# A two-layer attention and MLP kernel on one core: a new table of numbers for the planner that orders its instructions

## The chip, the cores and the metric

One Trainium2 chip, one NeuronCore. The metric is the device time of one execution in microseconds (us). The engines are named as the profile names them: PE (TensorE matmuls), PEld (TensorE weight loads), DVE (VectorE), ACT (ScalarE), POOL (GpSimd) and SP (SyncE, which issues DMAs).

## The reference

Two layers that share their weights, on x of 2048 rows by 448 columns in bf16. Each layer is an attention with 16 heads of 28 columns, and an MLP of 1792 hidden columns with a squared ReLU:

```python
def _A_ref(x, wqkv, wo):
    qkv = (x @ wqkv).reshape(B, S, 3, H, Dh).transpose(2, 0, 3, 1, 4)
    q, k, v = qkv[0], qkv[1], qkv[2]
    scores = jnp.einsum("bhqd,bhkd->bhqk", q, k) * Dh ** -0.5
    p = _softmax(scores, axis=-1)
    o = jnp.einsum("bhqk,bhkd->bhqd", p, v)
    return o.transpose(0, 2, 1, 3).reshape(B, S, D) @ wo

def _B_ref(x, w1, b1, w2, b2):
    r = relu(jnp.einsum("bsd,df->bsf", x, w1) + b1)
    return jnp.einsum("bsf,fd->bsd", r * r, w2) + b2

x = A_x
x = x + _A_ref(_layernorm(x), A_wqkv, A_wo)
x = x + _B_ref(_layernorm(x), B_w1, B_b1, B_w2, B_b2)
x = x + _A_ref(_layernorm(x), A_wqkv, A_wo)
x = x + _B_ref(_layernorm(x), B_w1, B_b1, B_w2, B_b2)
```

## The kernel before, in words

**The unit of work.** The exponentials are the bulk. The 2 x 16 x 2048 x 2048 scores are cut into 2048 *banks* of 128 keys (partitions) by 512 query columns in float32. The queries go in *blocks* of 256 rows; in the second layer the last 256 rows are two blocks of 128, here called block 7 and block 8. A *pass* is one block with one group of four heads, and each pass goes over all keys.

**Score groups.** `s_stream` issues a *score group*: up to three banks in one tile `sc` (two such tiles take turns), by matmuls of K_sb with Q_sb at L1360. Each bank of a group is of another head and so of other rows of the PE. ACT turns the banks of a group into `pt` with one ACTIVATE at L1403 (1536 columns for three banks, 1024 for two).

**Banks on DVE.** `apart` may give a bank to DVE. Usually it is the third one of a group, and then ACT gets two. A tile `sc` is free for a new group when ACT and DVE have both read it. DVE takes an exponential by integer arithmetic: one TENSOR_SCALAR out of `sc` (L1424, in `a_unit`), two *shifts* of what it made (L1440, in `a_rest`) and one addition (L1453). A shift may go to POOL or to DVE; `a_rest` names both engines, and the planner takes the one on which it would end first, with a handicap for DVE that numbers of the table set:

```python
t = Op(("POOL", "DVE"), (EDUR, TDUR), apiece, deps=[c], ...)
h = Op(("POOL", "DVE"), (EDUR, TDUR), other, deps=[c], ...)
t.aside = h.aside = lambda: TASIDE2 if pool_left[0] > PLIM or ... else TASIDE
```

A bank can also be a fourth one beside a group that keeps all three for ACT. It then lies in `mt`, one of the two PSUM tiles that the other matmuls use, and this is tried only when enough of them are free (`bank_free`, with the number MFREE):

```python
if len(us) == 3 and bank_free(o.start):
    j = apart(use(js), o.start, us, 0.0)      # own = True: four banks
if j is None and len(us) == 3 and THIRD:
    own = False                               # two for ACT, one for DVE
```

**The rest of the work**, on PE and DVE, lies between the score groups: `p_stream` multiplies `pt` by V_sb into `oT` (L1555); DVE and small DMAs divide by the row sums (L1625 to L1683); `chain` does the output projection (wo), the layernorm (L692, L697, L816, with a reciprocal root on POOL at L717), its transposes on PE (L756, copied by DVE at L768), the MLP (matmuls with w1 and w2 at L871, ReLU at L1763 on DVE or L1761 on ACT, square at L1770 or L1768, the sum to x at L1692), and for the first layer the second layer's K, Q and V (`qkv`, DVE at L972, L976 and L1006). A matmul with few rows can ride beside a score group in rows that it leaves free (L954). Where PE has room, a score group's matmuls are issued again, or an idle matmul (L1821) is put in.

**What sets the order.** A `Planner` runs when the program is built. It keeps a clock for each engine, takes at every step the operation that could start first (by priorities where several could), and so writes one fixed order for each engine. The chip only follows this order; waits are by semaphores. The planner's rules read some 60 numbers (C_PRIO, V_LATE, TASIDE, MFREE, MORE and so on). `s_stream` changes them on the way, at the score group whose number stands in the table `PACE`:

```python
gi = len(gbuf)
globals().update(PACE.get(gi, {}))
```

FORCE and SKIP in the table name single groups in which a bank must or must not go to DVE.

Of the kernel before, what the change touches and what calls it, by code (L numbers as in the profile page):

```python
# [180 lines left out]
SKIP = ()
PACE = {
    0: {'BUSY': 1.0, 'LOW': 0.7, 'CHUNK': 1, 'EV': 2.9, 'FAR': 6, 'KEEP': 5, 'LAG': 16, 'LEAD': 18, 'MARGIN':
         1.5, 'MORE': 3, 'PRE': 0.5, 'SLACK': 0.7, 'SPAN': 8, 'TB': 1.3, 'TB2': 3, 'V_AGE': 5, 'V_LAST': 3,
# [6 lines left out]
    16: {'PRE': 0, 'CHUNK': 3, 'PWAIT': 3},
    24: {'ASIDE': 0, 'TASIDE': 0.2, 'SKIP': (25,)},
    32: {'FORCE': (38,)},
    40: {'PLIM': 2, 'TASIDE': -0.2, 'XMIN': 3, 'SKIP': (47,)},
# [1 line left out]
    56: {'PWAIT': 0.6, 'V_LATE': 6},
    72: {'C_PRIO': 1.6},
    80: {'LOW': 0.5},
    88: {'TB': 1.6},
    96: {'CHUNK': 1, 'FORCE': (103,)},  # L200
    104: {'LEAD': 6},
    120: {'LAG': 1, 'SKIP': (120,)},
    128: {'CHUNK': 3, 'SKIP': (130,)},
    136: {'MARGIN': 3},
    160: {'SKIP': (161,)},
    168: {'GUEST': 1, 'FORCE': (172,)},
    176: {'GWAIT': 0.3, 'FORCE': (182,)},
    184: {'MMC': 0.46, 'SKIP': (185,)},
    192: {'GUEST1': 1, 'SKIP': (193,)},
    208: {'PMAX': 4, 'SKIP': (213,)},  # L210
    216: {'GNEXT': 0.3},
    232: {'PLIM': 4, 'FORCE': (239,)},
    240: {'GOPEN': 2},
    248: {'GUEST1': 0, 'FORCE': (253,)},
    264: {'FORCE': (270,)},
    272: {'NEAR_U': 0},
    288: {'SPARE': 5},
    296: {'PORTP': 2},
    304: {'LADD': 0.05, 'FORCE': (310,)},
    312: {'FORCE': (312,)},  # L220
    320: {'SKIP': (323,)},
    328: {'LADD': 0.1},
    336: {'HOLD': 3},
    352: {'PORTP': 0.3},
    360: {'GNEXT': 0.5, 'FORCE': (362,)},
    368: {'NEAR_U': 9, 'SKIP': (371,)},
    376: {'GWAIT': 1, 'PORTP': 0.1, 'SKIP': (383,)},
    392: {'PLIM': 2, 'FORCE': (394,)},
    400: {'BUSY': 1.05, 'V_PAST': 1, 'FORCE': (403,)},
    408: {'GUEST': 0},  # L230
    416: {'V_WAIT': 8},
    440: {'MORE': 1, 'FORCE': (445,)},
    448: {'TASIDE2': 0},
    456: {'TB2': 2.4},
    464: {'HOLD': 4, 'FORCE': (464,)},
    480: {'LADD': 0.2, 'BEHIND': 6},
    488: {'HOLD': 5, 'V_AGE': 3, 'PLIM': 6},
    496: {'C_PRIO': 2.6, 'RES': 1, 'PRE': 0.8},
    504: {'HOLD': 6, 'SPARE': 3, 'TASIDE': 0.2},
    512: {'FORCE': (515,)},  # L240
    520: {'NEAR': 3, 'SKIP': (524,)},
    528: {'V_AGE': 8, 'FORCE': (531,)},
    536: {'GOPEN': 0.2, 'FORCE': (536,)},
    552: {'BUSY': 1.0, 'FORCE': (556,)},
    560: {'VGAP': 0.08, 'GUEST': 1},
    568: {'LOW': 1.0},
    576: {'TB2': 3, 'FORCE': (581,)},
    584: {'V_PAST': 2, 'TB2': 1.6, 'V_WAIT': 3},
    592: {'RES2': 2, 'SOON': 0.3, 'FORCE': (594,)},
    600: {'FAR': 9, 'ASIDE': 0.2, 'FORCE': (605,)},  # L250
    608: {'GOPEN': 2, 'FORCE': (608,)},
    616: {'FAR': 6, 'FORCE': (619,)},
    624: {'V_LAST': 2.5},
    632: {'LAG': 3, 'RES': 3},
    648: {'MMC': 0.9},
    656: {'TASIDE2': -0.4},
# [1618 lines left out]
```

## Time and profile before

| | |
|---|---|
| three runs | 798.44, 799.81, 800.02 us; median 799.81 |
| the profiled execution | 799.5 us; its span from the first to the last instruction 797.7 us |
| busy in the span | PE 775.0, DVE 731.9, ACT 779.7, POOL 443.9 us |
| score groups on ACT (L1403) | 683: 318 of three banks, 365 of two |
| first group starts, last group ends on ACT | 9.58 us, 779.93 us |
| granted TensorE clock | 1.000 |

The profiled execution's own time is 1.8 us more than its span. A group's "busy" counts overlapping instructions once, and "mean ns" is the record of one instruction. Records of neighbours on DVE and on ACT overlap by some 0.1 us, so a record is longer than what an instruction costs in a full queue.

### The profile page before, as it was taken

Reading aid. Unit: us, or ns where it says so; the run is one execution under the profiler, and the core shown is the slowest. Engines: PE = TensorE matmul, PEld = TensorE weight load, DVE = VectorE, ACT = ScalarE, POOL = GpSimd, SP = SyncE. Lnnn points to the kernel's source line nnn. Section 1 sums busy time; section 2 is a strip of 40 time slices with the busy share of each in tenths; the row PEclk is TensorE's granted clock in tenths of the full one; section 3 lists DMA queues with packets and bytes.
Section 4 is the critical chain, followed back from the end, with each engine's and each line's share of the span. In section 5 each row is a group of like instructions: output and inputs, shape, how many; then the busy total and the mean of one; then the engine's idle time right before and its main releaser. Section 6 shows DMA issues by size and latency. Waiting matters only on the chain.

```text
span 797.7 us, 29438 instructions
## 1 busy us (share of the span) xinstructions
PE 775.0 (97%) x12386; PEld 418.1 (52%) x12386; DVE 731.9 (92%) x1673; ACT 779.7 (98%) x702; POOL 443.9 (56%) x704
## 2 busy tenths in 40 slices
PE   9999999999999999999999999989999999999998
PEld 6455545455454555455454544545454545555565
DVE  8899999989998979989998999899999999999663
ACT  8999999999999999999999999999999999999993
POOL 3365775745665645666665556465664565655310
PEclk9999999999999999999999999999999999999999
DMA  9200011000000000000000000011100000000000
GB/s 252 85 3 2 3 30 29 16 18 9 12 14 16 17 16 16 5 14 16 2 3 2 2 3 2 4 43 30 28 17 22 22 28 16 28 8 22 23 7 25
DMA packets 32482, 18.16 MB, mean 23 GB/s; under 512 B 17818, under 2 KB 31899, under 8 KB 32348
## 3 DMA queue, kind: packets, MB, share of 16 engines
q1 hardware_dynamic: 32204, 16.16, 7.3%
q8 instruction: 97, 1.59, 0.8%
q14 instruction: 37, 0.30, 0.1%
q10 hardware_dynamic: 144, 0.11, 0.0%
HBM read 13.98 MB, written 2.06 MB: 20 GB/s over the span
## 4 chain that ended last, share of the span: by engine, by line
PE 60%; DVE 17%; ACT 14%; issue 6%; DMA 1%; POOL 1%; ACTq 0%; SPq 0%; DVEq 0%; POOLq 0%
PE mt L871 26%; PE sc L1360 18%; ACT pt L1403 14%; PE oT L1555 13%; DVE pt L1424 5%; DVE pt L1453 2%; DVE r L1763 2%; PE mt L954 1%; PE tp L756 1%; DVE st L692 1%; PE sc L871 1%; DVE V_sb L1770 1%; DVE x_sb L1692 1%; DVE xn L816 1%; PE mt L890 1%
## 5 line engine op out<-in xcount | busy, mean ns | idle before, releaser
L1403 ACT ACTIVATE pt<-sc 128x1536 bf16<-128x1536 f32 (+1 forms) x683 | 767.1, 1261 | 3.8 <-PE sc L1360 2.7
L1360 PE MATMUL sc<-Q_sb,K_sb 32*128 32x256 bf16 (+1 forms) x4018 | 249.3, 268 | 12.2 <-ACT pt L1403 8.6
L1440 POOL TENSOR_SCALAR v_c<-pt 128x512 int16<-128x512 int16 x233 | 153.2, 658 | 96.6 <-DVE pt L1424 40.0
L1424 DVE TENSOR_SCALAR pt<-sc 128x512 int16<-128x512 f32 x277 | 188.7, 684 | 11.3 <-PE sc L1360 9.1
L1360 PEld LDWEIGHTS <-K_sb 32*128 32x128 bf16 x4700 | 102.2, 92 | 169.4 <-issue 102.0
L1555 PE MATMUL oT<-pt,V_sb 128*32 128x256 bf16 (+1 forms) x4168 | 184.7, 268 | 0.4
L1555 PEld LDWEIGHTS <-V_sb 128*32 128x32 bf16 x5104 | 119.1, 96 | 52.6 <-issue 48.7
L871 PE MATMUL mt<-xnT,w 128*128 128x256 bf16 (+1 forms) x904 | 120.7, 269 | 1.9 <-DVE xnT L768 1.0
L1440 POOL TENSOR_SCALAR K_sb<-pt 128x512 int16<-128x512 int16 x117 | 76.9, 657 | 60.2 <-DVE pt L1424 29.9
L871 PEld LDWEIGHTS <-w 128*128 128x128 bf16 x936 | 75.9, 97 | 37.7 <-issue 29.9
L1763 DVE TENSOR_SCALAR r<-mt 128x512 bf16<-128x512 f32 x106 | 72.4, 683 | 5.1 <-PE mt L871 4.4
L1440 POOL TENSOR_SCALAR V_sb<-pt 128x512 int16<-128x512 int16 x86 | 56.3, 654 | 32.5 <-DVE pt L1424 14.5
L1555 PE MATMUL oT<-v_c,V_sb 128*32 128x256 bf16 (+1 forms) x460 | 68.9, 271 | 0.1
L1453 DVE TENSOR_TENSOR pt<-pt,v_c 128x512 bf16<-128x512 bf16 x146 | 62.6, 437 | 2.2 <-POOL v_c L1440 1.8
L871 PE MATMUL mt<-w,V_sb 128*128 128x448 bf16 (+1 forms) x274 | 64.2, 350 | 0.0
L717 POOL TENSOR_TENSOR rstd<-mv,mhalf 128x2 f32<-128x2 f32 (+1 forms) x34 | 23.8, 700 | 38.2 <-DVE mv L699 21.2
L1440 POOL TENSOR_SCALAR v_c<-v_c 128x512 int16<-128x512 int16 x39 | 26.0, 668 | 25.3 <-DVE v_c L1424 13.9
L692 DVE BATCH_NORM_STATS2 st<-x_sb 128x6 f32<-128x448 bf16 x63 | 38.7, 615 | 0.8 <-DMA x_sb<-in_A_x_dram 0.6
L1692 DVE TENSOR_TENSOR x_sb<-x_sb,mt 128x448 bf16<-128x448 bf16 x60 | 36.6, 612 | 2.3 <-PE mt L871 2.0
L1360 PE MATMUL sc<-K_sb,K_sb 32*128 32x256 bf16 (+1 forms) x682 | 37.2, 250 | 0.7 <-ACT pt L1403 0.5
L871 PEld LDWEIGHTS <-V_sb 128*128 128x128 bf16 x302 | 23.4, 97 | 25.1 <-issue 11.6
L1555 PE MATMUL oT<-V_sb,V_sb 128*32 128x256 bf16 (+1 forms) x228 | 35.2, 273 | 0.1
(170 smaller groups left out, 945.7 us busy)
## 6 DMA issues: line engine op xcount, KB each, us to landing
rec<-scr SPq DMA_DIRECT2D x54, 128.0 KB
out_dram<-x_sb SPq DMA_DIRECT2D x15, 112.0 KB
x_sb<-in_A_x_dram SPq DMA_DIRECT2D x7, 224.0 KB
w<-in_B_w_dram SPq DMA_DIRECT2D x1, 1568.0 KB
w<-in_B_w_dram SPq DMA_DIRECT2D x1, 1344.0 KB
dn<-oT_sb SPq DMA_DIRECT2D x54, 4.0 KB
V_sb<-in_A_wqkv_dram SPq DMA_DIRECT2D x4, 168.0 KB
scr<-dn SPq DMA_DIRECT2D x27, 8.0 KB
```

The lines of the kernel that those rows point to most:

```text
L692: nc.vector.bn_stats(out=box["st"][:, :], in_=x_sb[:, t0 + j, :] if src is None else src())
L717: nc.gpsimd.tensor_tensor(out=rstd[:, a:b], in0=mv[0][:, a:b, 1], in1=mhalf[:, a:b], op=ALU.pow)
L756: nc.tensor.transpose(out=tp[:, dc, k * P:(k + 1) * P], in_=xn[:, dc * P:(dc + 1) * P], identity=ident[:, :])
L871: nc.tensor.matmul(box["t"][:, c0:c0 + n], lhsT=lhsT() if callable(lhsT) else lhsT, rhs=rhs, start=a and "x" not in rest, stop=b or stop is m)
L1360: nc.tensor.matmul(dst[k][:, i * nt * P:(i + 1) * nt * P], lhsT=K_sb[l][rows, g, (kb + i) * P:(kb + i + 1) * P], rhs=queries_of(l, g, t0, ...
L1403: t = nc.scalar.activation(out=pt[:, 0:n], in_=gbuf[gi]["sc"][:, 0:n], func=AF.Exp, scale=float(np.log(2.0)) * 2.0 ** -FRAC)
L1424: t = nc.vector.tensor_scalar(out=z.bitcast(DT.int16), in0=src, scalar1=EXP_BASE, scalar2=0.0, op0=ALU.add, op1=ALU.max)
L1440: (nc.vector if e == "DVE" else nc.gpsimd).tensor_scalar(out=box[k].bitcast(DT.int16), in0=gbuf[gi]["z"].bitcast(DT.int16), scalar1=1.0, s ...
L1453: (nc.vector if e == "DVE" else nc.gpsimd).tensor_tensor(out=z, in0=z, in1=box[1], op=ALU.add)
L1555: nc.tensor.matmul(box["t"][DHP * hh:DHP * hh + DHP, 0:n], lhsT=V_sb[l][:, tb, 4 * g + hh, :], rhs=p, start=hh in starts and j == begins[h ...
L1692: nc.vector.tensor_tensor(out=x_sb[:, tb, lo:hi], in0=x_sb[:, tb, lo:hi] if src is None else src[:, lo:hi], in1=t[:, 0:hi - lo], op=ALU.add)
L1763: nc.vector.tensor_scalar(out=r[:, 0:w], in0=t[:, 0:w], scalar1=0.0, scalar2=None, op0=ALU.max)
```

## The change

Only the table `PACE` differs, from the entry for group 0 on, and with it the order that the planner writes. No function changes. The table is 13 lines shorter, so that each later line has a number lower by 13 (L1403 is now L1390, L1424 is L1411, the shift L1440 is L1427, the addition L1453 is L1440, L1692 is L1679, L1770 is L1757, L1360 is L1347). The core of the diff:

```diff
     0: {'BUSY': 1.0, ...
-         1.5, 'MORE': 3, 'PRE': 0.5, ... 'ASIDE': 0.2, ...
+         1.5, 'MORE': 3, 'PRE': 0.3, ... 'ASIDE': 0, ...
-         'GUEST': 1, 'GUEST1': 0, ...
+         'GUEST': 0, 'GUEST1': 0, ...
-    8: {'NEAR': 6, 'GUEST': 0, 'C_PRIO': 2.6},
...
-    48: {'TASIDE': 0.8},
...
-    664: {'GOPEN': 0.2},
+    8: {'EPRIO': 1.3, 'KEEP': 4, 'CHUNK': 3},
...
+    64: {'TASIDE': 0.4, 'NEAR_U': 9},
+    72: {'TASIDE': 0},
+    80: {'MORE': 1},
...
+    528: {'MFREE': 0, 'FORCE': (532,)},
...
+    648: {'CHUNK': 3},
```

What the two programs hold, counted in their instructions:

| | before | after |
|---|---|---|
| score groups (ACTIVATE into pt) | 683 | 681 |
| of three banks / of two | 318 / 365 | 320 / 361 |
| banks on DVE (each one L1424 and one L1453) | 364 | 366 |
| of these beside three banks of ACT | 0 | 5 |
| shifts (L1440) on DVE / on POOL | 116 / 612 | 221 / 511 |
| score matmuls (L1360), with the repeated ones | 4700 | 4634 |
| matmuls at L871 / riders at L954 / L890 | 2119 / 79 / 44 | 2094 / 90 / 61 |
| ReLUs on DVE / on ACT | 107 / 6 | 106 / 7 |
| between bank 100 and bank 1200: banks on DVE | 200 | 213 |
| there: shifts on DVE | 41 | 131 |
| there: ReLUs on DVE | 56 | 53 |
| matmuls at L871 and L890 from bank 2000 on | 236 | 211 |

The order up to the 22nd score group is the same. The last K columns of the second layer (K_sb1 by L976, two instructions for the last block) are made on DVE after banks 1272 and 1308 before, and after banks 1299 and 1311 now; their first readers are banks 1316 and 1324.

DVE around bank 240, in the first layer. In before, all shifts of these banks are on POOL; `v_c`, `V_sb1` and `pt` hold the banks that DVE took:

```order
L1424 TENSOR_SCALAR V_sb1_106<-sc_2225 128x512
L1453 TENSOR_TENSOR v_c_115<-v_c_115,V_sb1_106 128x512
L1424 TENSOR_SCALAR v_c_115<-sc_2274 128x512
L972 TENSOR_SCALAR Q_sb_104<-mt_2235 128x2x256
L1424 TENSOR_SCALAR V_sb1_106<-sc_2292 128x512
```

The same place in the changed program:

```order
L1411 TENSOR_SCALAR V_sb1_106<-sc_2244 128x512
L1440 TENSOR_TENSOR v_c_115<-v_c_115,V_sb1_106 128x512
L1427 TENSOR_SCALAR v_c_115<-V_sb1_106 128x512 x2
L1440 TENSOR_TENSOR V_sb1_106<-V_sb1_106,v_c_115 128x512
L959 TENSOR_SCALAR Q_sb_104<-mt_2287 128x2x256
L1411 TENSOR_SCALAR v_c_115<-sc_2302 128x512
```

Both shifts of a bank (L1427, twice) now stand on DVE, between two banks that DVE takes out of `sc`.

PE at the first of the five groups with a fourth bank, in the second layer. Three banks go to `sc`, which ACT reads whole, the fourth to a tile `mt` (the end of a round of four is shown). Before has no such group:

```order
L1347 LDWEIGHTS K_sb1_103
L1347 MATMUL sc_13409<-K_sb0_102,K_sb1_103 128x256
L1347 LDWEIGHTS K_sb1_103
L1347 MATMUL mt_13410<-K_sb0_102,K_sb1_103 128x256
L858 LDWEIGHTS V_sb0_105
```

What moved: a bank that would have been the third of a group of two stands beside a group of three.

DVE at the end of before, from the layernorm of block 8 on (the 448 wide add from `mt_17998` is block 7's, the 256 and 192 wide ones are block 8's, `V_sb0` takes the squared ReLUs):

```order
L1712 CAST x_sb_92<-sc_17829 128x448
L1692 TENSOR_TENSOR x_sb_92<-x_sb_92,sc_17852 128x448
L816 TENSOR_SCALAR xn2_110<-x_sb_92,mv_17872,rstd_17899 128x448
L768 COPY xnT_17901<-sc_17905 128x4x128
L1763 TENSOR_SCALAR r_17941<-sc_17915 128x256
L1770 TENSOR_TENSOR V_sb0_105<-r_17961 128x512
...
L1692 TENSOR_TENSOR x_sb_92<-K_sb0_102,sc_18011 128x256
L1692 TENSOR_TENSOR x_sb_92<-K_sb0_102,mt_18026 128x192
L1692 TENSOR_TENSOR x_sb_92<-K_sb0_102,mt_17998 128x448
```

And now:

```order
L1699 CAST x_sb_92<-sc_17794 128x448
L803 TENSOR_SCALAR xn2_110<-x_sb_92,mv_17860,rstd_17867 128x448
L755 COPY xnT_17869<-sc_17882 128x4x128
L1679 TENSOR_TENSOR x_sb_92<-K_sb0_102,mt_17871 128x448
L1757 TENSOR_TENSOR V_sb0_105<-r_17919 128x512
...
L1679 TENSOR_TENSOR x_sb_92<-K_sb0_102,sc_17967 128x256
L1679 TENSOR_TENSOR x_sb_92<-K_sb0_102,mt_17982 128x192
```

Block 6's last add (`sc_17852`) is gone from this stretch, to before the last score group, and block 7's 448 wide add stands ahead of block 8's squares and no longer last. On PE the matmuls for them moved likewise: after block 8's w1 matmuls there stood 8 + 14 + 14 + 6 matmuls with w2, and now 14 + 14; block 7's 14 stand as 10 ahead of block 8's transposes and 4 behind them.

More of the change, by code (lines that the diff above doesn't have):

```diff
@@ L183 @@
     0: {'BUSY': 1.0, 'LOW': 0.7, 'CHUNK': 1, 'EV': 2.9, 'FAR': 6, 'KEEP': 5, 'LAG': 16, 'LEAD': 18, 'MARGIN':
-         1.5, 'MORE': 3, 'PRE': 0.5, 'SLACK': 0.7, 'SPAN': 8, 'TB': 1.3, 'TB2': 3, 'V_AGE': 5, 'V_LAST': 3,
-         'V_PAST': 2, 'C_PRIO': 1.2, 'V_PRIO': 6, 'V_LATE': 2.6, 'V_WAIT': 5, 'ASIDE': 0.2, 'XMIN': 4, 'HOLD':
-         6, 'LADD': 0.3, 'RES': 2, 'RES2': 3, 'TASIDE': 0.4, 'EPRIO': 2.6, 'SPARE': 8, 'NEAR': 3, 'SOON': 1.5,
+         1.5, 'MORE': 3, 'PRE': 0.3, 'SLACK': 0.7, 'SPAN': 8, 'TB': 1.3, 'TB2': 3, 'V_AGE': 5, 'V_LAST': 3,
@@ L187 @@
+         'V_PAST': 2, 'C_PRIO': 1.2, 'V_PRIO': 6, 'V_LATE': 2.6, 'V_WAIT': 5, 'ASIDE': 0, 'XMIN': 4, 'HOLD': 6,
+         'LADD': 0.3, 'RES': 2, 'RES2': 3, 'TASIDE': 0.4, 'EPRIO': 2.6, 'SPARE': 8, 'NEAR': 3, 'SOON': 1.5,
          'VGAP': 0.03, 'PWAIT': 0.3, 'PNEAR': 0.2, 'PORTP': 1, 'PLIM': 3, 'MFREE': 5, 'QDEF': 4, 'LAG2': 6,
-         'GUEST': 1, 'GUEST1': 0, 'GUESTB': 1, 'STEER': 1, 'GWAIT': 1, 'GOPEN': 0.8, 'QFAST': ([1, 0],),
+         'GUEST': 0, 'GUEST1': 0, 'GUESTB': 1, 'STEER': 1, 'GWAIT': 1, 'GOPEN': 0.8, 'QFAST': ([1, 0],),
@@ L189 @@
          'CPOOL': 0, 'CASIDE': 0.3, 'HEAT': 0.6, 'WINDOW': 3.4},
-    8: {'NEAR': 6, 'GUEST': 0, 'C_PRIO': 2.6},
[L191 to L194, printed above, removed]
-    48: {'TASIDE': 0.8},
[L196 to L256, printed above, removed]
-    664: {'GOPEN': 0.2},
+    8: {'EPRIO': 1.3, 'KEEP': 4, 'CHUNK': 3},
@@ new lines @@
+    24: {'PORTP': 0.3},
+    40: {'TASIDE': -0.2, 'SKIP': (42,)},
+    48: {'V_LATE': 6, 'CHUNK': 2, 'V_PAST': 1, 'FORCE': (49,)},
+    64: {'TASIDE': 0.4, 'NEAR_U': 9},
+    72: {'TASIDE': 0},
+    80: {'MORE': 1},
+    88: {'V_PRIO': 4, 'FORCE': (92,)},
+    96: {'VGAP': 0, 'GNEXT': 0.5, 'GUEST': 1},
+    104: {'V_WAIT': 3, 'BUSY': 1.05, 'FORCE': (109,)},
+    120: {'XMIN': 3},
+    128: {'SPARE': 5, 'GIDLE': 0.1},
+    136: {'MARGIN': 3, 'XMIN': 2},
+    152: {'LADD': 0.2},
+    168: {'C_PRIO': 2.1, 'LOW': 1.0, 'BEHIND': 3},
@@ new lines @@
+    176: {'V_AGE': 6, 'SOON': 0.3},
+    192: {'GUEST1': 1},
+    208: {'URGE': 6, 'KEEP': 7, 'MFREE': 1},
+    216: {'XMIN': 4, 'SKIP': (221,)},
+    224: {'PWAIT': 0.1},
+    232: {'TB': 2.4},
+    248: {'GUEST1': 0},
+    256: {'V_LATE': 3.5, 'FORCE': (261,)},
+    264: {'PMAX': 4, 'V_PAST': 3, 'C_PRIO': 1.2},
+    272: {'EPRIO': 4},
+    280: {'SKIP': (287,)},
+    288: {'GUEST': 0, 'LADD': 0.3},
+    296: {'RES2': 4, 'FORCE': (299,)},
+    312: {'V_WAIT': 8, 'TB': 3, 'V_PRIO': 6},
+    320: {'LAG': 1, 'C_PRIO': 2.6, 'SOON': 1.5},
@@ new lines @@
+    336: {'VGAP': 0.08, 'TASIDE': 0.2},
+    376: {'TB2': 2.4, 'GWAIT': 0.3},
+    384: {'GUEST': 1, 'TB2': 0.9},
+    392: {'PLIM': 6},
+    408: {'TB': 1.0},
+    416: {'SPAN': 20, 'V_LATE': 2.6, 'BUSY': 0.95},
+    424: {'V_PAST': 1, 'V_LAST': 2.5, 'FORCE': (426,)},
+    448: {'LAG': 8},
+    464: {'PRE': 1.2, 'LEAD': 6, 'STEER': 0},
+    472: {'V_LAST': 2.2},
+    480: {'LADD': 0.05, 'SKIP': (480,)},
+    512: {'CHUNK': 1},
+    520: {'SPARE': 0, 'PNEAR': 0.05, 'V_PAST': 3},
+    528: {'MFREE': 0, 'FORCE': (532,)},
@@ L258 @@
+    544: {'BEHIND': 0, 'NEAR': 9},
+    552: {'PWAIT': 0.3},
+    560: {'LADD': 0.1},
+    576: {'MFREE': 5, 'SKIP': (582,)},
+    584: {'BUSY': 1.0},
+    600: {'SOON': 0.6},
+    608: {'RES2': 2, 'ASIDE': 2, 'RES': 3},
+    624: {'RES2': 1, 'FORCE': (625,)},
+    632: {'C_PRIO': 2.1, 'V_LATE': 4.6, 'FORCE': (638,)},
+    640: {'VGAP': 0.03, 'FORCE': (640,)},
+    648: {'CHUNK': 3},
 }
```

## The prediction

> **What bounds the kernel now.** I read the page first.
>
> ```profile
> span 797.7 us, 29438 instructions
> PE 775.0 (97%) x12386; PEld 418.1 (52%) x12386; DVE 731.9 (92%) x1673; ACT 779.7 (98%) x702; POOL 443.9 (56%) x704
> PEclk9999999999999999999999999999999999999999
> PE 60%; DVE 17%; ACT 14%; issue 6%; DMA 1%; POOL 1%; ACTq 0%; SPq 0%; DVEq 0%; POOLq 0%
> L1403 ACT ACTIVATE pt<-sc 128x1536 bf16<-128x1536 f32 (+1 forms) x683 | 767.1, 1261 | 3.8 <-PE sc L1360 2.7
> ```
>
> Three engines are above 90%, so the share of busy time does not pick one, and the chain (fourth line) hops between them. The last line does: ACT's exponentials are busy for 767.1 us and idle for only 3.8 us ahead of them. From 9.58 to 779.93 us ACT does nothing else. The time is therefore a head of 9.6 us, the exponentials with the waits inside them, and a tail of 797.7 - 779.9 = 17.8 us. The groups by form give the price of an exponential.
>
> ```profile
> L1403 ACT ACTIVATE pt<-sc 128x1536 bf16<-128x1536 f32 x318 | 455.9, 1489 | 2.2 <-PE sc L1360 1.6 <-PE oT L1555 0.2
> L1403 ACT ACTIVATE pt<-sc 128x1024 bf16<-128x1024 f32 x365 | 365.6, 1062 | 1.7 <-PE sc L1360 1.1 <-ACT pt L1403 0.2
> ```
>
> 318 x 1.489 + 365 x 1.062 = 861.1 us of records fit into 767.1 us, so neighbours overlap by 94.0 / 683 = 0.138 us. A group of three banks costs 1.351 us, one of two 0.924 us.
>
> Then the stretches, with DVE beside ACT.
>
> ```profile
> core 0: us, PE busy (x) PEld busy (x) DVE busy (x) ACT busy (x) POOL busy (x), PEclk, DMA share, GB/s
> 40.00:440.00 400.00, 391.32 (x6084) 206.39 (x6086) 374.13 (x823) 398.59 (x357) 247.56 (x394) 1.00 0.05 12
> 440.00:720.00 280.00, 272.85 (x4289) 140.60 (x4281) 271.81 (x627) 279.41 (x257) 163.09 (x254) 1.00 0.07 18
> 560.00:720.00 160.00, 157.64 (x2460) 80.26 (x2452) 157.87 (x366) 159.60 (x148) 95.14 (x147) 1.00 0.07 21
> 120.00:160.00 40.00, 38.61 (x624) 20.41 (x619) 37.24 (x83) 39.09 (x36) 26.13 (x39) 1.00 0.08 22
> ```
>
> From 560 to 720 us DVE is busy 98.7% of the time and ACT idles 0.40 us in 160 (0.25%). From 40 to 440 us, most of the first layer, DVE is busy 93.5% and ACT idles 1.41 us in 400 (0.35%). A nearly full DVE has so far cost ACT nothing. The waits name the path by which it could.
>
> ```profile
> PEld L1360 <- DVE pt L1424: 13.1, 43, 0.9
> ACT pt L1403 <- PE sc L1360: 2.7, 7, 0.5
> ```
>
> A score group waits for DVE to have read its bank (43 times, 13.1 us), and ACT for the score group (2.7 us): most of the first wait is covered by the other `sc` tile, on which ACT works meanwhile.
>
> **The change, part by part.**
>
> *ACT's groups.* Two more groups of three and four fewer of two: 2 x 1.351 - 4 x 0.924 = -1.0 us, all on the path. One ReLU more on ACT lies in the tail, where ACT mostly waits.
>
> *The tail.* It is read in the timeline.
>
> ```profile
> 774.69 5.24 ACT L1403 ACTIVATE pt<-sc 128x1536 bf16<-128x1536 f32 x4
> 780.58 1.69 PE L871 MATMUL sc<-w,V_sb 128*128 128x448 bf16 x8
> ...
> 783.45 0.61 DVE L1712 CAST x_sb<-sc 128x448 bf16<-128x448 f32 x1
> ...
> 783.98 0.61 DVE L1692 TENSOR_TENSOR x_sb<-x_sb,sc 128x448 bf16<-128x448 bf16 x1
> ...
> 784.50 0.39 DVE L816 TENSOR_SCALAR xn<-x_sb,mv,rstd 128x448 bf16<-128x448 bf16 x1
> ...
> 784.95 0.40 PE L756 MATMUL sc<-ident,xn 128*128 128x128 bf16 x4 [0.28 <-DVE xn L816]
> ...
> 785.35 0.61 PE L871 MATMUL sc<-xnT,w 128*128 128x128 bf16 x8
> 785.39 0.42 DVE L768 COPY xnT<-sc 128x512 bf16<-128x512 bf16 x1 [0.49 <-PE sc L756]
> ...
> 785.87 1.07 PE L871 MATMUL mt<-xnT,w 128*128 128x128 bf16 x16
> ...
> 789.00 1.68 PE L871 MATMUL mt<-w,V_sb 128*128 128x448 bf16 x8
> ...
> 789.39 0.63 DVE L1770 TENSOR_TENSOR V_sb<-r 128x512 bf16<-128x512 bf16 x2 [0.41 <-ACT r L1761]
> 790.52 1.69 PE L871 MATMUL sc<-w,V_sb 128*128 128x256 bf16 x14
> 792.05 2.45 PE L871 MATMUL mt<-w,V_sb 128*128 128x192 bf16 x20
> 792.30 0.42 DVE L1692 TENSOR_TENSOR x_sb<-K_sb,sc 128x256 bf16<-128x256 f32 x1 [2.29 <-issue]
> 793.40 0.35 DVE L1692 TENSOR_TENSOR x_sb<-K_sb,mt 128x192 bf16<-128x192 f32 x1 [0.68 <-PE mt L871]
> 794.54 0.62 DVE L1692 TENSOR_TENSOR x_sb<-K_sb,mt 128x448 bf16<-128x448 f32 x1 [0.78 <-PE mt L871]
> ```
>
> Behind block 8's layernorm PE works without a break to 794.5, and the last add ends at 795.16; the remaining 2.5 us to 797.7 is the store. From 789.00 on PE does 8 matmuls for block 7 (to 790.52), 14 x 256 columns and 14 x 192 for block 8, and 6 more for block 7. The changed order keeps only the two fourteens there. The 256 wide ones can then start at 789.0, but the last two of them need the square that ends at 789.39 + 0.63 = 790.02. At (792.05 - 790.52) / 14 = 0.11 us each they end at about 790.6 and not at 792.05. The 192 wide ones take up to 793.40 - 792.05 = 1.35 us, and the last add 0.35 us: 792.3 in place of 795.16, a gain of 2.8 us. Against it: block 7's 14 matmuls now stand round block 8's transposes. The ten ahead take 10 x 0.21 (1.69 / 8) = 2.1 us, in the place that block 6's 14 leave, and end where the transposes could start. The four behind, 4 x 0.21 = 0.84 us, take the place of block 7's last w1 matmuls (785.35, 0.61 us, and three ahead of it) under the copy at 785.39; block 8's w1 then starts near 786.1 in place of 785.87, and I charge 0.2 us. Block 6's add at 783.98, which held `xn` back to 784.50, is gone as well, but `xn` then meets the ten matmuls on PE, so I count nothing for it. Tail: -2.8 + 0.2 = **-2.6 us**. The 25 matmuls that left the stretch from bank 2000 on are done earlier, beside ACT. There the 66 score matmuls that are no longer repeated make room for them.
>
> *The head* is the same order: 0.
>
> *Shifts and banks on DVE.* The rows that price them:
>
> ```profile
> L1424 DVE TENSOR_SCALAR pt<-sc 128x512 int16<-128x512 f32 x277 | 188.7, 684 | 11.3 <-PE sc L1360 9.1 <-ACT pt L1403 0.9
> L1453 DVE TENSOR_TENSOR pt<-pt,v_c 128x512 bf16<-128x512 bf16 x146 | 62.6, 437 | 2.2 <-POOL v_c L1440 1.8
> L1440 DVE TENSOR_SCALAR v_c<-pt 128x512 int16<-128x512 int16 x55 | 15.1, 292 | 0.0
> L1440 POOL TENSOR_SCALAR v_c<-pt 128x512 int16<-128x512 int16 x233 | 153.2, 658 | 96.6 <-DVE pt L1424 40.0
> ```
>
> On DVE neighbours overlap by 0.08 us (783.45 + 0.61 ends 0.08 behind the next start, 783.98), so a shift costs 0.21 us there. 105 more are 22 us, against 797.7 - 731.9 = 65.8 us of idle DVE, 26 us of it in the last 78 us where no shifts are left. Nothing waits for a shift but the addition and pt x V, which `p_stream` does many groups later. Its price on the path is that a bank's L1424, or a K copy, stands 0.2 us later in DVE's queue; and the spare `sc` tile covers that so long as DVE keeps up. In the first layer it barely does. Between banks 100 and 1200, about the window from 40 to 440, there are 90 more shifts (18.9 us), 13 more banks (13 x (0.684 + 0.437 - 0.16) = 12.5 us) and 3 ReLUs with squares fewer (-2.8 us): 374.1 + 28.6 = 402.7 us of DVE. ACT's part of it falls by 13 x (1.351 - 0.924) = 5.6 us to 393.0. Yet busy time counts the last 0.08 us of every record that is followed by idle, and this goes when the queue is full: if it is so for 120 of the 823 records, DVE needs 402.7 - 9.6 = 393.1 us and just fits. So the price is between 0 and 9.7 us; below nothing, ACT's own idle time, 3.8 us, could go. The nearest row, 560 to 720 us at 98.7%, shows none: I take 0.
>
> [...]
>
> *The second layer* gets 11 fewer of the DVE banks, which is inside ACT's -1.0.
>
> *Last K columns.* Their second copy is made at bank 1311 for a reader at 1324, 13 banks or 13 / 3 x 1.351 = 5.9 us at most ahead; before it was 16. Behind two DVE instructions that is enough: 0, at worst +1.5 (two L1424 and an addition, less their overlap).
>
> Sum: 799.5 - 1.0 - 2.6 = **795.9 us** from the profiled execution, which lies 0.3 us below the median of the three runs, 799.81.
>
> **The rivals.**
>
> *DVE becomes the bound of the first layer* (slower). If DVE's 402.7 us overlap as little as now, ACT waits for scores whose `sc` tile DVE has not read, and loses up to 9.7 us: 805.6. The deciding point is DVE's need against 393 us. Half of it gives 800.7, the form in which I expect it. For it: the sum is over 100% by busy time. Against it: the full stretches of now. Chance 0.24.
>
> [...] POOL's shifts and DVE's additions read SBUF together. The addition takes 437 ns in the row above; with 101 shifts fewer on POOL additions could be shorter, DVE would get slack and ACT's 3.8 us of idle would shrink: 795.9 - 3.8 = 792.1. Chance 0.08. [...]
>
> *K comes late at the layers' boundary*: +1.5, 797.4. Chance 0.10.
>
> *The tail's matmuls come back in the stream* (the change does not do what it seems to). PE is busy 97%. If the moved matmuls push scores, the 2.6 us return: 798.5. Against it: 66 repeated matmuls fewer. Chance 0.08.
>
> **How the numbers follow.** The forecast, 795.9, has 0.50, with its own range of 794 to 798 for waits that shift by 2 us either way. Range: from 792.5, just above the port's case, to 801.0, past half of the DVE case; the upper half of it and a bit below stay out, under 0.2. About 0.2% (1.6 us) is what a measurement of this kernel can tell from no change, so below 798.2 is faster. Faster: 0.46 of the forecast, 0.08 port, 0.07 of K late: 0.61. Slower: 0.21 of the DVE case and 0.01 of the rest: 0.22. The same: 0.17.
>
> **What would show it.** Right: ACT's last exponential ends some 1 us earlier, near 779; the last add comes about 12.4 us behind it; L1403 (then L1390) keeps an idle time near 4 us; DVE is busy near 755 us. Wrong: the waits of PEld at the scores for DVE grow well past 13.1 us and ACT's idle time from 40 to 440 us past 1.4 us (the DVE case); the additions' mean falls towards 420 ns (the port); ACT waits near bank 1316 (K); or the stretch from 640 us to the last group gets longer per bank (the tail's matmuls).

## The result, and the profile after

| | before | after |
|---|---|---|
| median of 6 runs each, side by side | 799.41 us | 794.87 us |
| lowest to highest | 798.44 to 800.29 us | 794.63 to 796.85 us |
| ratio after / before | | 0.9948, 95% interval 0.9935 to 0.9961 |
| profiled execution / its span | 799.5 / 797.7 us | 794.63 / 792.7 us |
| first score group starts, last one ends | 9.58, 779.93 us | 9.42, 777.79 us |
| last score group's end to the end of the span | 17.8 us | 14.9 us |

The changed kernel is faster by 4.5 us; the forecast was 3.6 us in the profiled execution. The 5.0 us less in the span divide as the prediction divided them: head -0.2, the stretch of the exponentials -2.0 (770.35 to 768.38 us), tail -2.9.

The page of the kernel after: its span, the busy line, the shares of the chain, and the group of the exponentials.

```profile
span 792.7 us, 29225 instructions
PE 768.7 (97%) x12325; PEld 414.9 (52%) x12325; DVE 749.1 (95%) x1781; ACT 778.5 (98%) x701; POOL 378.6 (48%) x603
PE 51%; DVE 26%; ACT 15%; issue 6%; DMA 1%; POOL 1%; SPq 0%; DVEq 0%; ACTq 0%; POOLq 0%
L1390 ACT ACTIVATE pt<-sc 128x1536 bf16<-128x1536 f32 (+1 forms) x681 | 765.6, 1264 | 2.8 <-PE sc L1347 1.3
```

The chain's share on DVE rose from 17% to 26%, which looks as if DVE had become a bound. The last line says otherwise: ACT idles 2.8 us ahead of the exponentials, 1.0 us less than before (0.53 us of before's 3.8 lie ahead of its first group, none of after's 2.8). The groups by form hold the counts that the prediction priced, at durations within 2 ns of before.

```profile
L1390 ACT ACTIVATE pt<-sc 128x1536 bf16<-128x1536 f32 x320 | 457.7, 1490 | 1.6 <-PE sc L1347 1.0 <-PE oT L1542 0.2
L1390 ACT ACTIVATE pt<-sc 128x1024 bf16<-128x1024 f32 x361 | 360.8, 1064 | 1.2 <-PE sc L1347 0.3 <-ACT pt L1390 0.3
```

The windows of the kernel after show the first layer, where DVE got its extra work, and two stretches of the second.

```profile
core 0: us, PE busy (x) PEld busy (x) DVE busy (x) ACT busy (x) POOL busy (x), PEclk, DMA share, GB/s
40.00:440.00 400.00, 390.73 (x6111) 205.51 (x6109) 396.34 (x947) 398.40 (x362) 210.45 (x336) 1.00 0.05 12
440.00:720.00 280.00, 272.12 (x4224) 141.43 (x4223) 269.63 (x622) 279.49 (x251) 136.27 (x212) 1.00 0.07 19
```

From 40 to 440 us DVE is busy for 396.3 us of 400 (374.1 before), and ACT idles 1.60 us. That is 0.2 us more than before, but no difference: in the five experiments below that keep this stretch as it is (4 to 8), ACT idles between 1.35 and 1.69 us. In the waits of the kernel after, the path by which DVE could stop ACT became shorter, not longer (13.1 and 2.7 us before).

```profile
PEld L1347 <- DVE pt L1411: 9.5, 26, 1.2
ACT pt L1390 <- PE sc L1347: 1.3, 5, 0.5
```

The timeline of the tail, after:

```profile
769.48 8.31 ACT L1390 ACTIVATE pt<-sc 128x1536 bf16<-128x1536 f32 x6
780.28 2.06 PE L858 MATMUL mt<-w,V_sb 128*128 128x448 bf16 x10
781.75 1.17 DVE L803 TENSOR_SCALAR xn<-x_sb,mv,rstd 128x448 bf16<-128x448 bf16 x1
781.75 1.03 POOL L1721 TENSOR_TENSOR K_sb<-x_sb,K_sb 128x448 f32<-128x448 bf16 x1
782.97 0.40 PE L743 MATMUL sc<-ident,xn 128*128 128x128 bf16 x4 [0.63 <-DVE xn L803]
783.20 0.92 PE L858 MATMUL mt<-w,V_sb 128*128 128x448 bf16 x4
783.96 1.06 PE L858 MATMUL sc<-xnT,w 128*128 128x128 bf16 x16
...
787.09 1.69 PE L858 MATMUL sc<-w,V_sb 128*128 128x256 bf16 x14
788.62 1.32 PE L858 MATMUL mt<-w,V_sb 128*128 128x192 bf16 x14
789.98 0.35 DVE L1679 TENSOR_TENSOR x_sb<-K_sb,mt 128x192 bf16<-128x192 f32 x1 [0.68 <-PE mt L858]
```

The ten and the four matmuls for block 7 stand round block 8's transposes (780.28 and 783.20), and behind block 8's w1 only its own two fourteens are left, with one add behind them. One thing is new: `xn`, 0.39 us before, takes 1.17 us, beside an addition on POOL that starts at the same 781.75.

### The profile page after: what moved, and what is told of

It is laid out like the page before. It is cut to its first block, busy times and chain, and to the rows that moved or that the text cites. A ratio compares the mean times of both kernels' runs of the same rounds, so it can differ in the third digit from the quotient of the medians.

```text
span 792.7 us, 29225 instructions
## 1 busy us (share of the span) xinstructions
PE 768.7 (97%) x12325; PEld 414.9 (52%) x12325; DVE 749.1 (95%) x1781; ACT 778.5 (98%) x701; POOL 378.6 (48%) x603
## 4 chain that ended last, share of the span: by engine, by line
PE 51%; DVE 26%; ACT 15%; issue 6%; DMA 1%; POOL 1%; SPq 0%; DVEq 0%; ACTq 0%; POOLq 0%
PE mt L858 20%; ACT pt L1390 15%; PE sc L1347 15%; PE oT L1542 12%; DVE pt L1411 6%; DVE pt L1440 3%; DVE r L1750 2%; DVE v_c L1411 2%; DVE x_sb L1679 1%; PE mt L941 1%; PE tp L743 1%; DVE st L679 1%; DVE v_c L1440 1%; DVE v_c L1427 1%; DVE xn L803 1%
## 5 line engine op out<-in xcount | busy, mean ns | idle before, releaser
L1390 ACT ACTIVATE pt<-sc 128x1536 bf16<-128x1536 f32 (+1 forms) x681 | 765.6, 1264 | 2.8 <-PE sc L1347 1.3
L1347 PE MATMUL sc<-Q_sb,K_sb 32*128 32x256 bf16 (+1 forms) x3934 | 248.1, 268 | 13.3 <-ACT pt L1390 10.4
L1347 PEld LDWEIGHTS <-K_sb 32*128 32x128 bf16 x4634 | 99.5, 92 | 171.8 <-issue 107.0
L1411 DVE TENSOR_SCALAR pt<-sc 128x512 int16<-128x512 f32 x200 | 136.3, 685 | 2.8 <-PE sc L1347 2.0
L1427 POOL TENSOR_SCALAR v_c<-pt 128x512 int16<-128x512 int16 x148 | 96.1, 649 | 71.4 <-DVE pt L1411 34.3
L858 PE MATMUL mt<-xnT,w 128*128 128x256 bf16 (+1 forms) x888 | 117.9, 270 | 1.3 <-DVE r L1750 0.6
L858 PE MATMUL mt<-w,V_sb 128*128 128x448 bf16 (+1 forms) x288 | 67.3, 350 | 0.0
L1427 POOL TENSOR_SCALAR K_sb<-pt 128x512 int16<-128x512 int16 x68 | 45.3, 667 | 45.3 <-DVE pt L1411 33.2
L1427 POOL TENSOR_SCALAR v_c<-v_c 128x512 int16<-128x512 int16 x63 | 41.5, 658 | 43.2 <-DVE v_c L1411 23.9
L1427 POOL TENSOR_SCALAR V_sb<-pt 128x512 int16<-128x512 int16 x56 | 37.5, 670 | 44.8 <-DVE pt L1411 20.2
L1411 DVE TENSOR_SCALAR v_c<-sc 128x512 int16<-128x512 f32 x84 | 57.3, 682 | 0.0
L1440 DVE TENSOR_TENSOR pt<-pt,v_c 128x512 bf16<-128x512 bf16 x113 | 48.3, 432 | 0.5
L1347 PE MATMUL sc<-K_sb,K_sb 32*128 32x256 bf16 (+1 forms) x690 | 39.8, 249 | 1.8 <-ACT pt L1390 1.6
L1542 PE MATMUL oT<-V_sb,V_sb 128*32 128x256 bf16 (+1 forms) x276 | 39.7, 273 | 0.0
L1679 DVE TENSOR_TENSOR x_sb<-x_sb,mt 128x448 bf16<-128x448 bf16 x61 | 37.3, 611 | 1.5 <-PE mt L858 1.4
```

Source lines behind the costliest of these rows:

```text
L858: nc.tensor.matmul(box["t"][:, c0:c0 + n], lhsT=lhsT() if callable(lhsT) else lhsT, rhs=rhs, start=a and "x" not in rest, stop=b or stop is m)
L1347: nc.tensor.matmul(dst[k][:, i * nt * P:(i + 1) * nt * P], lhsT=K_sb[l][rows, g, (kb + i) * P:(kb + i + 1) * P], rhs=queries_of(l, g, t0, ...
L1390: t = nc.scalar.activation(out=pt[:, 0:n], in_=gbuf[gi]["sc"][:, 0:n], func=AF.Exp, scale=float(np.log(2.0)) * 2.0 ** -FRAC)
L1411: t = nc.vector.tensor_scalar(out=z.bitcast(DT.int16), in0=src, scalar1=EXP_BASE, scalar2=0.0, op0=ALU.add, op1=ALU.max)
L1427: (nc.vector if e == "DVE" else nc.gpsimd).tensor_scalar(out=box[k].bitcast(DT.int16), in0=gbuf[gi]["z"].bitcast(DT.int16), scalar1=1.0, s ...
L1440: (nc.vector if e == "DVE" else nc.gpsimd).tensor_tensor(out=z, in0=z, in1=box[1], op=ALU.add)
```

## The experiments

Each experiment is the changed kernel with one edit, and is compared with the kernel before on its own chip. For the changed kernel itself that ratio is 0.9948.

### 1. All shifts on POOL

```diff
-        (nc.vector if e == "DVE" else nc.gpsimd).tensor_scalar(
+        nc.gpsimd.tensor_scalar(
```

> The changed kernel, but all 221 shifts that stand on DVE are issued on POOL, at the same places of the order; PE and ACT keep their order. DVE loses some 221 x 0.21 = 46 us, POOL gains 221 x 0.66 = 145 us (379 to 524 of 793). Theory (the added shifts on DVE cost nothing on the path): within 1 us of the changed kernel, 794 to 796, unless POOL is now late for the additions, then slower. Rival (a full DVE holds up the score groups in the first layer): faster by 2 us or more, and ACT's idle time from 40 to 440 us falls well under 1.6 us.

Measured: 832.74 us, ratio 1.0412 (1.0398 to 1.0426). DVE has 221 instructions fewer and the kernel is 38 us slower. The waits of this run name the reason:

```profile
DVE pt L1440 <- POOL v_c L1427: 20.3, 26, 1.4
PEld L1347 <- DVE pt L1411: 34.7, 66, 1.8
ACT pt L1390 <- PE sc L1347: 21.0, 42, 1.8
```

The order on each engine is fixed, and where it puts a shift on DVE the addition stands close behind. With the shift on POOL that addition waits (first row), the next bank's L1411 waits behind the addition, a score group waits for that bank (second row, 9.5 us in the kernel after), and ACT for the group (third row). Two more things are mixed into the 38 us: the additions took 481 ns on average in place of 428, and the granted clock fell four times in the profiled execution (mean 0.992). So this is no clean test of DVE's load. It shows that in this order the shifts are needed where they are, and that short waits in DVE's queue, 1.4 us at most, can stop ACT.

### 2. More shifts on DVE

In the first layer every third shift of POOL goes to DVE, 104 more.

```diff
+    third = [0]
...
+        if e == "POOL" and gi < 400:
+            third[0] += 1
+            e = "DVE" if third[0] % 3 == 0 else e
```

> The changed kernel, but in the first layer (groups below 400) every third shift that stands on POOL is issued on DVE: 104 more there, 104 x 0.21 = 21.8 us, nearly all in the window from 40 to 440 us, where DVE is busy 396.3 of 400 us. Theory (the change has brought DVE just to its limit): DVE becomes the bound, 13 to 18 us slower than the changed kernel, 808 to 813 us, with ACT idle and PE's waits for L1424's successor grown. Rival (busy time overstates DVE, and much room is left): under 5 us slower.

Measured: 816.87 us, ratio 1.0215 (1.0201 to 1.0229), 22.0 us above the changed kernel. The same windows row and waits as above, in this run:

```profile
40.00:440.00 400.00, 378.28 (x5828) 198.26 (x5827) 397.78 (x993) 387.83 (x344) 142.88 (x228) 1.00 0.05 12
PEld L1347 <- DVE pt L1411: 20.5, 52, 1.3
ACT pt L1390 <- PE sc L1347: 12.5, 30, 1.1
```

DVE is busy 397.8 us of 400, hardly more than in the changed kernel, and ACT now idles 12.2 us there. 22.0 us for 104 shifts are 0.21 us each (0.20 by the one run whose clock stayed at 1.000, 815.87 us): every shift is paid in full at the price that the prediction used, a record of 0.29 less an overlap of 0.08 us. The cost lies where the shifts do: between banks 100 and 1200, where 99 of them stand, 404.9 us became 425.1. So the changed kernel leaves DVE no room in the first layer. The expectation was low because it left some room. As in experiment 1 the order was not planned anew; that DVE is busy for all but 2.2 of 400 us says that its load is the bound here, and not single waits.

### 3. Shorter additions

The opposite: the first layer's additions take 128 of 512 columns, some 40 us less for DVE. The kernel leaves out the last term for three quarters of each of these banks.

```diff
+            n = 128 if gi < 400 else 512
             # both operands and the result: [:, 0:n]
```

> The changed kernel, but in the first layer (groups below 400) DVE's additions (L1453 of before) go over 128 of 512 columns; the rest of the bank stays without its last term. That takes some 0.2 us from each of about 220 additions, 40 us of DVE, and changes no order. Theory (DVE is at its limit in the first layer but does not hold up ACT): at most 1 us faster, 793.9 to 795. Rival (DVE shares the bound there): 2 to 5 us faster, ACT's waits and the length of its records fall.

Measured: 794.31 us, ratio 0.9934 (0.9923 to 0.9946). The windows row:

```profile
40.00:440.00 400.00, 391.07 (x6132) 205.91 (x6132) 367.50 (x951) 399.10 (x363) 203.49 (x336) 1.00 0.05 12
```

DVE's busy time falls from 396.3 to 367.5 us and ACT's idle time from 1.60 to 0.90 us. In the changed kernel DVE holds ACT up by about 0.7 us in this stretch (0.8 by the highest of the idle times given above), against the 9.7 us of the case in which DVE is the bound. Experiments 2 and 3 together: DVE is full to the brim, and not over it.

### 4. Block 7's matmuls at the end again

The 14 matmuls of block 7 that the change put round block 8's transposes go back behind block 8's w1 matmuls, where before had them; the last 12 of them end up behind everything.

```diff
+            if (l, qb) == (1, len(blocks[1]) - 1):
+                yield Op("-", 0.0, None, deps=[o], sets=["w1end"])
+            if (l, qb) == (1, len(blocks[1]) - 2):
+                yield Op("-", 0.0, None, deps=["w1end"])
             # ahead of the w2 matmuls
```

> The changed kernel with the tail of before: block 7's 14 matmuls with w2 wait until block 8's w1 matmuls are issued, as in before. Only the end of PE's and DVE's order changes. Theory (the tail's gain is that these 14 left its end): 14 x 0.21 = 2.9 us more at the end, less up to 0.4 us ahead of the transposes: +2.5 to +2.9, 797.4 to 797.8 us. Rival (the gain comes from another place, the tail is held by the squares or the store): under 1 us slower.

Measured: 799.6 us, ratio 0.9994 (0.9984 to 1.0004), 4.7 us above the changed kernel; the last score group ends at 777.62 us, so all of it is in the tail, 19.4 us long. The matmuls come back as expected (timeline):

```profile
790.18 1.32 PE L858 MATMUL mt<-w,V_sb 128*128 128x192 bf16 x14
791.34 2.43 PE L858 MATMUL sc<-w,V_sb 128*128 128x448 bf16 x12
```

From 791.34 to the end of PE are 2.4 us. The other 2 us stand in the windows of this run. PEclk is the third number from the end.

```profile
780.30:782.80 2.50, 0.01 (x1) 0.01 (x1) 2.23 (x5) 0.83 (x3) 1.58 (x2) 1.00 0.00 0
782.80:787.10 4.30, 3.78 (x39) 3.61 (x40) 0.85 (x2) 0.60 (x1) 0.00 (x0) 0.60 0.01 4
```

With the ten matmuls gone, PE has nothing to do for 2.5 us while block 8's layernorm runs, and in the next 4.3 us the granted clock is 0.60 on average (0.50 for 3.41 us from 783.32 on, and 1.00 around that). In the changed kernel it is 1.00 there. The expectation knew nothing of that.

### 5. The same with idle matmuls in the hole

Experiment 4 with ten idle matmuls of the same size where the ten were.

```diff
+            def idle(e):
+                t = bank(idle_o, "mt")
+                for _ in range(10):
+                    nc.tensor.matmul(t[:, 0:D], lhsT=ident, rhs=xns[0][:, 0:D], ...)
+            idle_o = Op("PE", 1.9, idle, deps=[o], acq=R_m)
...
```

> The kernel with block 7's w2 matmuls late, and ten idle matmuls of 448 columns in the hole that this leaves on PE ahead of block 8's transposes (their result is not used). With the hole, PE was idle for 2.5 us, the granted clock was 0.60 from 782.8 to 787.1 us, and the time 799.6 us, 4.7 us more than the changed kernel and not 2.5 to 2.9. Theory (two parts: 14 matmuls at the end, 2.9 us, and a clock that falls after the hole, some 1.8 us): the clock stays 1.00, 797.5 to 798.0 us. Rival (the 4.7 us have another cause): stays near 799.6.

Measured: 797.53 us, ratio 0.998 (0.9971 to 0.999). In the five of nine runs whose mean clock was 0.999 or 1.000 it was 797.11 to 797.53, in the middle 797.18; of the other four, the profiled one lost the clock in the stream, at 526.75 us, and the rest have no trace. In the tail of the profiled one the clock (third number from the end) stayed up:

```profile
782.80:787.10 4.30, 3.15 (x40) 2.26 (x38) 2.02 (x3) 0.67 (x2) 1.57 (x2) 1.00 0.01 4
```

The changed kernel's five runs at 1.000 have 794.77 in the middle, and the seven of experiment 4 at 0.998, which is one drop of 3.4 us, have 799.18. So the way from the one to the other is 2.4 us for the matmuls and 2.0 us for the clock. The traces divide it a little differently: from the last exponential to the end of the last add there are 12.5 us in the changed kernel, 15.4 here and 16.8 in experiment 4, which makes 2.8 and 1.4 us. What the ten matmuls do, beside being done, is to keep the clock up. That the hole was the cause is shown: filling it with work of no use brings the clock back.

### 6. No fourth banks

No bank is taken as a fourth one beside three, from group 528 on (316 groups of three, 367 of two).

```diff
-            if len(us) == 3 and bank_free(o.start):
+            if False:
```

> The changed table without groups of a fourth bank: the planner goes on from group 528 with groups of two and of three (316 of three, 367 of two; 366 banks on DVE as before). Two adds of w2 now stand late in the tail again (block 6's ahead of the transposes, block 7's at the very end). Theory (a fourth bank has no worth of its own, its part is that the work behind it comes out in an order with a shorter tail): ACT's exponentials the same within 1 us, tail as in before, +2.5 to +3.5: 797.4 to 798.4 us. Rival (the fourth banks carry the gain in the stream): the last exponential ends 2 us or more later.

Measured: 799.75 us, ratio 1.0005 (0.9996 to 1.0014): the whole gain is gone. But the last score group ends at 777.56 us, as in the changed kernel (777.79). All that is lost is in the tail, 19.7 us long, as its timeline shows:

```profile
788.58 2.85 PE L858 MATMUL sc<-w,V_sb 128*128 128x256 bf16 x28
791.26 2.81 PE L858 MATMUL mt<-w,V_sb 128*128 128x448 bf16 x14
794.11 0.62 DVE L1679 TENSOR_TENSOR x_sb<-K_sb,mt 128x448 bf16<-128x448 f32 x1 [2.29 <-PE mt L858]
```

Without these five banks the planner's clocks run differently from group 528 on, and block 7's w2 stands last, all 14 matmuls of it (6 in before, whose tail is 17.8 us). The fourth banks are worth nothing as exponentials: at 1.351 and 0.924 us the groups of this run add up to 766.0 us and those of the changed kernel to 765.9. That they bring the order of the tail with them is what the change got from them.

### 7. The new table for the first layer only

The changed entries up to group 447, the old ones from 448.

```diff
-    448: {...}   # and all later entries of after
+    448: {...}   # every number set to what before has there; then before's entries
```

> The changed table up to group 447, the old one from group 448 on (the first layer's order of the change, the second layer planned by the old numbers). 316 groups of three and 367 of two, 0.9 us of ACT less than before by 1.351 and 0.924 us each; the tail has its two late adds as in before. Theory (the gain is ACT's sum and the tail, wherever in the stream the banks are moved): 799.4 - 0.9 - 1 for waits + 0 for the tail = 797.5 to 799 us. Rival (the first layer's order is the gain, 5.5 us between bank 100 and 1200): 794 to 795 us.

Measured: 806.92 us, ratio 1.0099 (1.0085 to 1.0112), slower than both kernels. The windows of this run:

```profile
40.00:440.00 400.00, 390.86 (x6123) 205.64 (x6121) 396.57 (x949) 398.65 (x362) 209.51 (x335) 1.00 0.05 12
440.00:720.00 280.00, 269.92 (x4166) 138.87 (x4159) 256.39 (x589) 277.21 (x248) 136.44 (x214) 1.00 0.07 19
```

The first layer is the changed one (ACT idles 1.35 us). With the old numbers behind it, ACT idles 2.79 us from 440 to 720 us, where both kernels have 0.5 to 0.6, and the tail is 23.5 us long, 8.6 us more than in the changed kernel. So the parts of the table don't add up: each number was found for the state in which the planner stands there. How the old numbers come to leave so much for the tail was not followed up.

### 8. POOL's addition behind the layernorm

The addition on POOL at 781.75 makes K_sb, which is first needed at block 8's last adds. Here it waits for `xn`; no engine's order changes.

```diff
+            norms[t0 + j] = nc.vector.tensor_scalar(...)
...
+            t = nc.gpsimd.tensor_tensor(...)
+            if end: follows(t, norms[t0], "behind the layernorm")
```

> The changed kernel with one wait more: POOL's 448 wide add for block 8 (K_sb, at 781.75 us) waits for DVE's xn, which starts at the same time. In the trace of after this xn takes 1.17 us in place of 0.39. Theory (the two hold each other up): xn takes 0.39 again, the transposes start when PE is done with the ten w2 matmuls (782.35 in place of 782.97), 0.6 us faster, 794.2 to 794.4 us. Rival (xn is long for another reason, or the path runs elsewhere): no change.

Measured: 794.22 us, ratio 0.9929 (0.9917 to 0.9942), tail 14.2 us. The interval overlaps that of the changed kernel; the timeline decides.

```profile
782.12 0.40 DVE L803 TENSOR_SCALAR xn<-x_sb,mv,rstd 128x448 bf16<-128x448 bf16 x1
782.57 0.40 PE L743 MATMUL sc<-ident,xn 128*128 128x128 bf16 x4
782.66 1.03 POOL L1722 TENSOR_TENSOR K_sb<-x_sb,K_sb 128x448 f32<-128x448 bf16 x1 [0.58 <-DVE xn L803]
```

`xn` is back at 0.40 us, 0.77 us less, and the transposes follow it 0.45 us behind its start in place of 1.22. The tail is shorter by the same amount, 14.16 in place of 14.92 us. This is the fastest version of all by its median.

### 9. No repeated score matmuls, and two mixtures

The score matmuls that are issued again where PE has room are left out (4352 in place of 4634).

```diff
-            for i in list(range(4)) * (again + 1):
+            for i in range(4):
```

> The changed kernel without the repeated score matmuls: 4352 in place of 4634 (before had 4700); nothing else moves in any engine's order. Theory (the repeats stand only where PE would idle, so 66 more or fewer move no time, as long as the clock holds): 794 to 796 us, the granted clock 1.00. Rival (the repeats keep the clock up, and the change had it near the edge): half-clock stretches of 3.4 us as in the late-w2 kernel, some 1.5 to 2 us for each, 797 us or more. Third (they held up real work on PE): 1 us or more faster.

Measured: 795.09 us (792.26 to 798.63), ratio 0.9934 (0.9913 to 0.9955). The time goes with the mean clock of the run: 792.26 and 793.09 us at 1.000, 794.75 and 795.43 at 0.998, 796.91 at 0.994, 798.63 at 0.991. In the profiled one the clock fell twice between 520 and 545 us. This row, and that of the changed kernel below it:

```profile
520.00:545.00 25.00, 22.43 (x312) 10.45 (x302) 21.15 (x52) 21.44 (x20) 10.67 (x16) 0.80 0.13 35
520.00:545.00 25.00, 22.59 (x364) 11.64 (x362) 24.43 (x58) 25.00 (x24) 12.68 (x19) 1.00 0.13 35
```

ACT loses 3.6 us in these 25. Where the clock stays up the repeats cost some 2 us, by two runs of this kernel. They seem to pay for that by making drops rarer: the mean clock was 0.999 or more in 26 of 37 runs of the kernels that keep them all (the changed kernel and experiments 3, 5, 6 and 8), and in 2 of 6 here. Two mixtures with experiment 8's edit tried to have both:

```diff
-            for i in list(range(4)) * (again + 1):
+            for i in list(range(4)) * (again * (400 <= gi < 520) + 1):   # the first
+            for i in list(range(4)) * (again * (gi >= 360) + 1):         # the second
```

> The changed kernel with block 8's add on POOL behind xn (0.65 us faster alone), and with repeated score matmuls only in groups 400 to 519 (9 repeats kept of 47). Without any repeats the time was 792.3 to 793.1 us where the clock held, and 794.8 to 798.6 where it fell to half for 3.4 us or more near 526 to 540 us. Theory (the repeats cost some 2 us where PE has real work, and are needed only round the layers' boundary): 791.5 to 792.7 us with a clock of 1.00. Rival (any place may lose the clock without them): spread of several us, median 794 or more.

> The changed kernel with block 8's add on POOL behind xn, and without the repeated score matmuls of groups 0 to 359 alone (4514 score matmuls in place of 4634); all later ones stay. In the two kernels with fewer repeats the clock fell only behind 520 us, where this one keeps them. Theory (repeats cost time in the first layer and hold the clock in the second): clock 1.00, 793.0 to 793.7 us, under the 794.2 of the same kernel with all repeats. Rival (the repeats of the first layer cost nothing): 794.0 to 794.6.

Measured: 794.64 us, ratio 0.9938 (0.9924 to 0.9952), and 795.19 us, ratio 0.9942 (0.9926 to 0.9958). Neither beats experiment 8. In the first, the clock fell in every run (mean 0.998 or 0.996), in the profiled one at 720.6 us, where its repeats are left out. In the second it stayed at 1.000 in two of six (793.27 and 793.96 us), though no repeat was taken away where the profiled one lost it, at 535 us. So the repeats do not ensure the clock, and how much they help it is not shown.

## Why the prediction was right, point by point

- **ACT's groups, -1.0.** Right as a term: two more of three and four fewer of two, at 1.490 and 1.064 us a record. The stretch became 2.0 us shorter: the groups' busy time fell by 1.5 us (767.1 to 765.6), as their records also overlap by a little more (0.140 against 0.138 us), and ACT's idle time between the first group and the last by 0.5 (3.3 to 2.8). The prediction had put the waits between 0 and 9.7 us of loss, with a gain of up to 3.8 as the other bound, and took 0.
- **The first layer, by counts.** From the start of the group that holds bank 100 to that of bank 1200, 410.4 us became 404.9: 5.5 us, against the predicted 13 x 0.427 = 5.6. From there to the last score group's end 316.6 became 320.4. DVE's extra work was thus all but free.
- **DVE as the bound, the slower rival.** Refuted for this kernel: DVE's own load costs ACT some 0.7 us (experiment 3). But it was a near thing: 104 more shifts cost 22 us (experiment 2). The prediction set the work between banks 100 and 1200 against the window from 40 to 440 us, which is 10 us shorter than that stretch. The stretch itself, before and after:

```profile
52.86:463.25 410.39, 401.87 (x6287) 212.79 (x6286) 383.84 (x845) 408.98 (x367) 252.70 (x401) 1.00 0.04 12
52.50:457.37 404.87, 395.57 (x6172) 208.13 (x6165) 401.04 (x952) 403.27 (x368) 213.08 (x339) 1.00 0.05 12
```

  DVE's busy time rose by 17.2 us, not by the 28.6 of the plain sum, and stayed 3.8 us inside the stretch. The prediction's argument, that busy time counts overlaps that vanish in a full queue, 9.6 us in all, is borne out: added up one by one, DVE's records there went from 443.2 to 476.7 us, 33.5 more, so their overlaps grew by 16.3. Of these the 107 new records explain 8.6 at 0.08 each, and 7.7 are left for the old ones. Shorter additions gave another 3 us (see the shorter additions below), which the sum did not have. With DVE 99% busy in this stretch its load did not yet set the time (experiment 3); with 104 shifts more it did (experiment 2).
- **The tail, -2.6.** Measured -2.9, and the last add ends 12.5 us behind the last exponential, where the sum gives 12.6 (the 12.4 among the prediction's signs leaves out its own charge of 0.2). The main term holds: putting block 7's 14 matmuls back costs 2.4 us by the times and 2.8 by the traces (experiments 4 and 5), and 2.8 was predicted. That the rest fits as well is luck, since two things were not in it and nearly cancel. With block 6's add gone, `xn` starts 3.96 us behind the last exponential in place of 4.57, 0.6 us earlier; the prediction counted nothing for this. And `xn` takes 0.8 us longer, as it collides with POOL's addition; without the collision the tail is 0.8 us shorter still (experiment 8). The prediction had counted on the transposes to wait for the ten matmuls, and they waited for `xn`. A third thing was not in it either: the ten matmuls also keep the clock up. That is no gain over before, whose tail ran at 1.00 too, but the same hole left empty would have cost 1.4 to 2.0 us.
- **The head.** Left as it was by the prediction; it became 0.2 us shorter. The first group starts between 9.09 and 9.79 us in the traces of the experiments, so this is no more than scatter.
- **Shorter additions, the faster rival ("port" in the prediction's sums).** No run shows a port; what the traces of before and after show is that an addition can be longer when it starts while a shift runs on POOL. In before the 152 additions with no shift on POOL beside them take 415 ns on average and at most 444, and of the 212 others 32 take more than 500 ns, up to 849; after, 19 of 169 do. All 51 start while a shift runs on POOL, none ahead of it. The rival's sign came, its time did not. Between banks 100 and 1200 the additions' mean fell from 436 to 421 ns, where the prediction named 420, and with all shifts on POOL it rose to 481 in place of the changed kernel's 428 (experiment 1). That is 3 us of DVE, but it went into DVE's own extra work: ACT's idle time shrank by 0.5 us and not by 3.8. No run varies POOL's shifts alone.
- **K late; the tail's matmuls come back in the stream.** Neither is in the trace: ACT's waits for scores are 1.3 us in the whole kernel, and fewer than before.

## What to carry to other kernels

Price an engine that takes on work by what its queue has left in that stage, and price each instruction at its record less its overlap: up to the brim the work was all but free, and past it each shift cost its full 0.21 us. In a tail, look for what stands last on the busiest engine and move it into the hole where that engine waits for a short chain; here this also kept the clock up, at 1.00 where the hole left empty had 0.60. And don't judge the parts of a schedule found by search one by one: half of this table was slower than either whole.

## What the runs showed of the hardware that was not expected

- **The clock fell after a hole in PE's work.** After a hole of 2.5 us on PE the granted clock averaged 0.60 over 4.3 us (experiment 4), and this cost 1.4 to 2.0 us; with ten idle matmuls in the hole it did not fall (1.00, experiment 5), nor in the changed kernel, where PE is busy for 2.04 of the 2.60 us from 780.30 on. Where it falls inside the stream, one drop costs about 2 us too: the changed kernel's five runs at 1.000 are 794.63 to 795.22 us, and its one at 0.998 is 796.85. In the traces the drops go to 0.50 and last 3.4 or 6.8 us: in the profiled run of experiment 9 the clock averages 0.83 from 524 to 534 us and 0.76 from 534 to 548, which is 3.4 and 6.7 us at 0.50. Averages over 25 us do not tell a stretch with drops from one without: in the rows of experiment 9 PE is busy for 22.43 us at a mean clock of 0.80 and for 22.59 us at 1.00. What decides whether a gap in PE's work brings the clock down no run of this case separates.
- **POOL's addition can hold up DVE.** `xn` took 1.17 us beside a POOL addition that starts with it, and 0.40 us when the addition came behind it (experiment 8). In the changed kernel and in experiments 4, 5 and 7, where the two start within 0.01 us of one another, `xn` takes 1.16 or 1.17 us; where it starts 0.16 us ahead (before, and experiment 6) it takes 0.39, and the addition 1.12 in place of 1.03. There it is the later of the two that is the longer, by 0.09 us. Why `xn`, which starts with an addition of 1.03 us, takes 0.77 us more no run here shows. The prediction had weighed such a delay for the additions, not here, where it decided 0.8 us.
